# Last block of x turned as a full tile; SyncE's turns and loads planned with other durations

## Chip, cores, metric

One core of one Trainium2 chip. The metric is the device time of one launch in microseconds (us), lower is better; a kernel's figure is the median of its runs.

## The reference

Causal attention by blocks of 64 positions, and behind it a feed-forward layer with a swish. Inputs are f32.

```python
# q, k, v: (8 batches, 8 heads, 576 positions, 64)
scores = where(block_i >= block_j, q @ k.T / 8, -1e9)      # blocks of 64 positions
attn   = softmax(scores) @ v
x      = attn.transpose(0, 2, 1, 3).reshape(4608, 512)     # 8 * 576 rows, 8 * 64 columns
h      = x @ w_in                                          # (4608, 2048)
g      = h / (1 + exp(-beta * h))
out    = g @ w_out                                         # (4608, 512)
```

## The kernel before

**Units and row blocks.** The attention is cut into 32 units: unit u = 4b + c is the pair c of heads of batch b. The feed-forward layer is cut into nine row blocks r of 512 rows of x. A batch has 576 rows, so row block 3 (rows 1536 to 2047) needs all four units of batches 2 and 3, row block 4 those of batches 3 and 4, and so on.

**What a unit does.** Its q and k are loaded in f32 (L622 for the first two batches, L658 for the others, where one load brings two units), cast to bf16 by POOL (L629, L669) and turned so that the head dimension lies on the partitions: for batches 0 and 1 by TensorE (PE, L638) with a copy by VectorE (DVE), for batches 2 to 7 by one DMA transpose a pair of units, issued by SyncE (SP, L676). In this text that is a *q/k turn*, T0 to T11: T0 is for units 8 and 9, T1 for 10 and 11, and so on to T11 for 30 and 31. The pieces of v of a batch are loaded by SP too (L552, L555; six a batch from batch 1 on, the fifth and the sixth a quarter as large) and cast by POOL (L578, four casts a batch). Then come the scores on PE (L712, with a few at L443; from batch 2 on in three groups for two units: the first half of the first unit, a joint group, the first half of the second unit), the exponentials on ScalarE (ACT, L728 and L740), zeros into masked corners (DVE, L734 and L736), the product with v on PE (L768, 30 matmuls, here *AV*), and its division by the row sums on DVE (L780, L787), which gives x for the unit.

**How x gets its place.** x has 576 rows a unit and must be turned as well. For batches 0 to 2 (units 0 to 11) PE does it with five transposes (L817), the fifth of 64 rows. DVE or ACT copies the result to `xT`. For units 12 to 31 a DMA transpose on SP does it (L804), in one or two pieces: an *x turn*. Row block r on PE starts when the x of all its units is in `xT`.

**A row block.** Sixteen groups of four matmuls (L1004, 128x512 each) give h; each is followed by a tanh on ACT (L1014) and a product on DVE (L1018) that leaves g in `gT`. Row block 0 has plain output products (L1040, sixteen groups of four matmuls). Row blocks 1 to 8 use a Strassen-like form with 14 groups of eight matmuls of 256 columns (L925), whose sums of operands DVE makes (L889).

**What sets the order.** Nothing of this order stands in the code by hand. Every piece of work is an operation given to a planner with `P.op(engine, duration, emit, deps, tiles, prio, xfer=...)`. `Plan.schedule` (L85) plays the whole program through with these durations: at each moment an engine that is free takes the ready operation of best priority. For a DMA, `dur` is the time for which the issuing engine is held, `xfer` is the time that its data take in the ring of its queue, and the landing is put at the end of the transfer plus a constant (`LAND`, 2600 ns). An issue of SP that finds more than `RING` = 6000 ns of transfers ahead holds SP for longer (L269). What comes out is one fixed list for each engine, and each engine runs its list in order, waiting at semaphores. A duration that is changed therefore can change the place of every operation behind it, on all engines. Between the loads an order of their own is fixed (L842 to L851): q and k by units, and v of a batch behind its second pair of units.

**Buffers that matter here.** `ST` (four half buffers for q/k loads), one buffer of raw v for batches 2 to 7, two of cast v, three of `QKT`, three of `xq` (x before it is turned; the AV of unit u needs the x turn of unit u - 3 to have landed), and the eight banks of PSUM.

Of the kernel before, what the change touches and what calls it, by code (L numbers as in the profile page):

```python
# [359 lines left out]
def bass_blockwise_causal_attn__then__act_swish_beta_kernel(  # L360
# [10 lines left out]
    with es:  # L371
# [32 lines left out]
        xq = [sb(f"xq{i}", [128, 5, 128], bf16) for i in range(3)]  # L404
# [3 lines left out]
        identB = sb("identB", [128, 128], bf16)  # L408
# [8 lines left out]
        PSb = PS[:].rearrange("p b n -> p (b n)").bitcast(bf16).rearrange("p (b n) -> p b n", b=8)  # L417
# [3 lines left out]
        P = Plan()  # L421
# [16 lines left out]
        def pr(u):  # L438
            b, c = divmod(u, NPAIR)
            return u if b < 1 else 10 * u if b < 2 else 994 + 100 * (b - LAG) + 4.9 * c  # L440
# [11 lines left out]
        def xq_(tx):  # L452
            return 3 if tx.cls == "XX" else tx.slot
# [16 lines left out]
        for i in range(NQ):  # L470
# [5 lines left out]
            o = P.op("POOL", 200, mk(lambda g, i=i: g.memset(Vn[i][:, 4, :, 64:66], 0.0)), prio=-5)  # L476
# [6 lines left out]
        for i in range(NQ, NE + 1):  # L483
# [4 lines left out]
                  xfer=100, dma=("d_beta", 1), prio=0.1)  # L488
# [3 lines left out]
                  deps=[bt, c2], tiles=[tb], lat=400, mode="full", prio=5)  # L492
# [24 lines left out]
        for i in range(NFILL):  # L517
# [14 lines left out]
            n = 125  # L532
            o = P.op("PE", n, ff, deps=[c2, c4], tiles=[tf], lat=n, mode="full", prio=1e6 + i)
# [6 lines left out]
        for b in range(B):  # L540
            ts, t = P.tile("Vs"), P.tile("V")
# [3 lines left out]
            for h0, h1, e, tt in PARTS[b]:  # L545

                vs = []
                for i in tt:
                    def fv(g, e, ts=ts, t=t, b=b, h0=h0, h1=h1, i=i):
                        d = Vn[t.slot] if e == "POOL" else Vs[ts.slot]  # L550
                        if i < 4:
                            return [g.dma_start(d[:, i, h0:h1, 0:64],  # L552
                                                v[b, h0:h1, 128 * i:128 * i + 128, :].rearrange("h p d -> p h d"))]
                        o = i - 4
                        return [g.dma_start(d[64 * o:64 * o + 64, 4, h0 + o:h1:2, 0:64],  # L555
                                            v[b, h0 + o:h1:2, 512:576, :].rearrange("h p d -> p h d"))]

                    n = (h1 - h0) / 8 * (1 if i < 4 else 0.25)
                    if e == "SP":
                        o = P.op("SP", 300 + 550 * n, fv, tiles=[ts], xfer=1400 * n,  # L560
                                 prio=3.5 + 0.1 * (h0 > 0) if b == 0 else 4 * b + (3.5 if b < 2 else 0.5),
                                 dma=["d_V", h0, 1])
                    else:
                        o = P.op("POOL", 150 + 1450 * n, fv, tiles=[t], xfer=1400 * n, prio=-30 if b == 0 else 4 * b + (3.5 if b < 2 else 0.5), dma=["d_VP", h0, 1])
                        o.after = lastv if b else None
                    vs.append(o)
# [6 lines left out]
                n = 5 if 4 in tt else len(tt)  # L573
# [27 lines left out]

        xt = []
        early6 = []
        QKI, QKX = 550, 2700
        for u in range(NU):
            b, c = divmod(u, NPAIR)
            Tv = tl[b]
# [44 lines left out]
            elif p == 0:  # L652
# [23 lines left out]
                    return [g.dma_start_transpose(QKT[td.slot][:].rearrange("c a w (t n) -> c (a w t) n", n=128),  # L676
                                                  QKn[tn.slot][:].rearrange("p a w n -> p (a w n)")[:, 0:2560])]

                turned = [P.op("SP", 3250, ft, deps=casts, tiles=[tt_, tn], xfer=3200, prio=-1, dma=["d_T", 0, 1])]
            tqk, cps = tt_, turned  # L680
            ex = []
            zs = []
# [130 lines left out]

            def fx(g, e, tx=tx, px=px):
                for i in range(5):
                    r = 128 if i < 4 else 64
                    z = g.transpose(PSb[:, px.slot, 128 * i:128 * i + r], xq[xq_(tx)][0:r, i, :], identB[0:r, 0:r])  # L817
                return z

            xp = P.op("PE", 5 * 66, fx, deps=nrm, tiles=[tx, px], lat=5 * 66 + 170, mode="full", prio=pr(u)+.5 + 5 * (b < 1))  # L820

            def fy(g, e, px=px, c=c, b=b):
                for t0, n, x0 in pieces(b):
# [310 lines left out]
```

## Time and profile before

| what | us |
|---|---|
| median of 3 runs | 333.13 |
| lowest, highest run | 331.49, 333.41 |
| the profiled execution, its own time | 331.63 |
| its span, first to last instruction | 329.8 |
| PE busy in it | 318.9 (97%) |
| DVE, ACT, POOL busy | 223.9, 212.6, 87.1 |

The profile is of one execution at a granted TensorE clock of 1.000. A line of its views gives the start, the duration, the engine, the source line, the operation, and tiles as out<-in; what stands in brackets is idle time of the engine ahead of the group and what ended it. SPq is SyncE's sequencer, which issues DMAs; the duration there is that of the issue, not of the transfer.

### The profile page before, as it was taken

The numbers are of one execution on the slowest core, as the hardware profiler recorded it, in microseconds if no ns is written. First come the engines' busy times: TensorE is split into PE (matmuls) and PEld (weight loads), VectorE is DVE, ScalarE is ACT, GpSimd is POOL, SyncE is SP. The second block draws the span as 40 slices with busy tenths as digits, with TensorE's granted clock in tenths as the row PEclk, the third lists the DMA queues.
The fourth block names the chain that finished last, engine by engine and source line by source line (L and its number), as shares of the span: only waits on it lengthen the run. The fifth ranks groups of instructions, "written<-read, shape, count | busy, mean of one in ns | idle before, by whom it ended". The sixth has DMA issues, their size and how long they took to land.

```text
span 329.8 us, 7390 instructions
## 1 busy us (share of the span) xinstructions
PE 318.9 (97%) x3111; PEld 198.2 (60%) x3003; DVE 223.9 (68%) x448; ACT 212.6 (64%) x324; POOL 87.1 (26%) x127
## 2 busy tenths in 40 slices
PE   7999999999999999999999998999999999999996
PEld 1364455445687457855666655576566766666685
DVE  4848875678654899449957795678477685666742
ACT  2876974397557976678577675974876554544521
POOL 7756181065073045104530730250000000000000
PEclk9999999999999999999999999999999999999999
DMA  8999999999999999989989999969002320100023
GB/s 206 229 243 236 192 218 205 215 275 196 209 276 190 246 198 189 230 178 203 188 188 191 264 223 151 219 121 165 33 34 42 98 39 32 66 32 34 6 92 127
DMA packets 154993, 53.41 MB, mean 162 GB/s; under 512 B 139072, under 2 KB 154448, under 8 KB 154960
## 3 DMA queue, kind: packets, MB, share of 16 engines
q1 hardware_dynamic: 141200, 40.19, 64.5%
q0 software_dynamic: 5568, 4.36, 8.5%
q10 hardware_dynamic: 8192, 8.39, 8.0%
q8 instruction: 24, 0.39, 0.5%
q14 instruction: 9, 0.07, 0.1%
HBM read 36.71 MB, written 9.44 MB: 140 GB/s over the span
## 4 chain that ended last, share of the span: by engine, by line
PE 83%; ACT 4%; DVE 3%; POOL 3%; SPq 2%; DMA 2%; issue 2%; POOLq 0%; ACTq 0%
PE PS L1004 36%; PE PS L925 28%; PE PS L768 8%; PE PS L712 6%; PE PS L1040 4%; ACT E L728 3%; DMA Vs<-in_v_dram 2%; SPq L552 2%; DVE gT L1018 1%; POOL QKn L629 1%; ACT th L1014 1%; PE PS L817 1%; DVE OV L889 1%; PE PS L638 0%; POOL w_in L502 0%
## 5 line engine op out<-in xcount | busy, mean ns | idle before, releaser
L1014 ACT ACTIVATE th<-PS,beta 128x512 f32<-128x512 f32 x144 | 96.5, 700 | 60.3 <-PE PS L1004 59.1
L1004 PE MATMUL PS<-xT,w_in 128*128 128x512 bf16 x542 | 130.2, 379 | 3.7 <-ACT E L728 1.2
L1018 DVE SCALAR_TENSOR_TENSOR gT<-th,PS 128x512 f16<-128x512 f32 x144 | 95.1, 682 | 30.2 <-ACT th L1014 29.3
L728 ACT ACTIVATE E<-PS 128x1024 bf16<-128x1024 f32 x93 | 92.1, 1029 | 26.1 <-PE PS L712 25.7
L1004 PEld LDWEIGHTS PS<-xT,w_in 128*128 128x128 bf16 x576 | 53.2, 98 | 56.9 <-DVE gT L1018 2.5
L925 PE MATMUL PS<-w_out,gT 128*128 128x256 f16 x512 | 63.0, 273 | 0.0
L925 PEld LDWEIGHTS PS<-w_out,gT 128*128 128x128 f16 x512 | 49.0, 98 | 12.2 <-issue 1.5
L578 POOL CAST Vn<-Vs 128x640 bf16<-128x640 f32 (+1 forms) x28 | 22.4, 800 | 97.4 <-DMA Vs<-in_v_dram 96.1
L669 POOL CAST QKn<-ST 128x640 bf16<-128x640 f32 x48 | 37.9, 790 | 23.7 <-DMA ST<-in_q_dram 13.8
L712 PE MATMUL PS<-QKT 64*128 64x512 bf16 (+4 forms) x328 | 33.8, 295 | 0.4 <-ACT E L740 0.2
L768 PEld LDWEIGHTS PS<-Vn,E 128*128 128x128 bf16 x930 | 31.0, 97 | 4.3 <-issue 0.4
L946 ACT ACTIVATE ost<-PS 128x512 f32<-128x512 f32 x32 | 19.4, 606 | 21.7 <-PE PS L925 21.7
L925 PE MATMUL PS<-OV 128*128 128x256 f16 x256 | 32.0, 273 | 0.5 <-DVE OV L889 0.5
L768 PE MATMUL PS<-Vn,E 128*128 128x65 bf16 x930 | 32.0, 193 | 0.3 <-POOL Vn L578 0.3
L712 PEld LDWEIGHTS PS<-QKT 64*128 64x128 bf16 (+1 forms) x328 | 13.3, 96 | 27.0 <-issue 7.8
L925 PEld LDWEIGHTS PS<-OV 128*128 128x128 f16 x256 | 24.1, 98 | 6.5 <-issue 0.8
L787 DVE TENSOR_TENSOR xq<-PS,inv 128x640 bf16<-128x640 f32 x30 | 24.7, 822 | 0.8
L889 DVE TENSOR_TENSOR OV<-gT 128x1024 f16<-128x1024 f16 x32 | 24.0, 757 | 1.1 <-PE PS L925 0.6
L734 DVE MEMSET E<- 64x64 uint32 x62 | 6.9, 112 | 20.5 <-ACT E L728 18.3
L949 DVE SCALAR_TENSOR_TENSOR ost<-PS,ost 128x512 f32<-128x512 f32 x22 | 15.2, 689 | 8.2 <-PE PS L925 5.8
L925 PE MATMUL PS<-OV,gT 128*128 128x256 f16 x128 | 16.1, 273 | 0.0
L1040 PE MATMUL PS<-w_out,gT 128*128 128x512 f16 x64 | 15.5, 380 | 0.0
(64 smaller groups left out, 175.3 us busy)
## 6 DMA issues: line engine op xcount, KB each, us to landing
out_dram<-ost ACTq DMA_DIRECT2D x32, 256.0 KB, 2.9
ST<-in_q_dram SPq DMA_DIRECT2D x12, 576.0 KB, 6.2
ST<-in_k_dram SPq DMA_DIRECT2D x12, 576.0 KB, 7.6
Vs<-in_v_dram SPq DMA_DIRECT2D x24, 256.0 KB, 4.5
ST<-in_q_dram SPq DMA_DIRECT2D x8, 288.0 KB, 6.5
ST<-in_k_dram SPq DMA_DIRECT2D x8, 288.0 KB, 7.0
w_in<-in_moe_w_in_dram POOLq DMA_DIRECT2D x4, 512.0 KB, 10.1
w_out<-in_moe_w_out_dram POOLq DMA_DIRECT2D x4, 512.0 KB, 9.9
```

Of the source, the lines that this page charges most:

```text
L578: return g.tensor_copy(Vn[t.slot][:, 0:n, g0:g1, 0:64], Vs[ts.slot][:, 0:n, g0:g1, :])
L669: return g.tensor_copy(QKn[tn.slot][:].rearrange("p a w n -> p (a w n)")[:, 640 * (2 * a + w):][:, 0:640] .rearrange("p (t h d) -> p t h d ...
L712: z = g.matmul(o, QKT[tqk.slot][r, uu % 2, 1, 128 * t + y:128 * t + m + y], x)
L728: return g.activation(E3[es_(te)][:, g0, :, :], PS[:, ps.slot:ps.slot + 2, :], ACT.Exp, scale=0.125)
L768: z = g.matmul(o, eblk(te, t, i, h), Vn[Tv.slot][:, t, 2 * c + h, 0:65], start=(t == 0), stop=(t == i))
L787: return g.tensor_tensor(xq[xq_(tx)][:].rearrange("p i (h d) -> p h i d", h=2), both(pv, 0, 64), x, ALU.mult)
L889: return P.op("DVE", dve_t(SZ * HC / 2), mk(lambda g: g.tensor_tensor(fo(), fx(), fy(), op)), deps=deps, tiles=tiles, prio=prio)
L925: x = g.matmul(PS[:, pw.slot, HM * w:HM * w + HM], fa()[:, j, 128 * w:128 * w + 128], fb()[:, j, :], start=first and (pair or w == 0) and ...
L1004: z = g.matmul(PS[:, ph.slot, :], w_in[:, c, 128 * j:128 * j + 128], xT[:, c, row % RX:row % RX + RC], start=(c == 0), stop=(c == 3))
L1014: return g.activation(th[tt.slot][:], PS[:, ph.slot, :], ACT.Tanh, scale=beta[:, j:j + 1])
L1018: return g.scalar_tensor_tensor(out=gT[tg.slot][:, j, :], in0=th[tt.slot][:], scalar=1.0, in1=PS[:, ph.slot, :], op0=ALU.add, op1=ALU.mult)
L1040: z = g.matmul(PS[:, po.slot, 0:d1 - d0], gT[tg.slot][:, j, 128 * w:128 * w + 128], w_out[:, j, d0:d1], start=(j == 0), stop=(j == NJ - 1))
```

## The change

Four numbers of the planner and one piece of code.

- The fifth transpose of an x tile on PE (units 0 to 11) takes all 128 rows instead of 64. Only the first 64 columns of its result are used, as before. The planner's duration goes from 5 x 66 to 5 x 57 ns.
- A q/k turn: SP is held for 4200 ns instead of 3250, and its transfer takes 2600 ns instead of 3200.
- A q/k load of two units (`QKX`): its transfer takes 2300 ns instead of 2700.
- A whole piece of v (256 KB) from batch 1 on: 1100 ns instead of 1400.

```diff
-                        o = P.op("SP", 300 + 550 * n, fv, tiles=[ts], xfer=1400 * n,
+                        o = P.op("SP", 300 + 550 * n, fv, tiles=[ts], xfer=(1400 if b < 1 else 1100) * n,
...
-        QKI, QKX = 550, 2700
+        QKI, QKX = 550, 2300
...
-                turned = [P.op("SP", 3250, ft, deps=casts, tiles=[tt_, tn], xfer=3200, prio=-1, dma=["d_T", 0, 1])]
+                turned = [P.op("SP", 4200, ft, deps=casts, tiles=[tt_, tn], xfer=2600, prio=-1, dma=["d_T", 0, 1])]
...
             def fx(g, e, tx=tx, px=px):
                 for i in range(5):
-                    r = 128 if i < 4 else 64
-                    z = g.transpose(PSb[:, px.slot, 128 * i:128 * i + r], xq[xq_(tx)][0:r, i, :], identB[0:r, 0:r])
+                    z = g.transpose(PSb[:, px.slot, 128 * i:128 * i + 128], xq[xq_(tx)][:, i, :], identB[:])
                 return z

-            xp = P.op("PE", 5 * 66, fx, deps=nrm, tiles=[tx, px], lat=5 * 66 + 170, mode="full", prio=pr(u)+.5 + 5 * (b < 1))
+            xp = P.op("PE", 5 * 57, fx, deps=nrm, tiles=[tx, px], lat=5 * 57 + 170, mode="full", prio=pr(u)+.5 + 5 * (b < 1))
```

What comes out of the planner differs as follows. PE's list is the same, but for the fifth transposes, up to the 13th h group of row block 0 (43.6 us in the profile before); there the AVs of units 4 and 5 come two h groups earlier. SP's list is the same up to the third of the six pieces of v of batch 2; from there on:

```
SP before: v (third) | T0 | v x3 | q k q k | v | T1 | v v | T2 | v x3 | q k q k | v | T3 | v | T4 | x12 | v x4 | q | x13 | k q | x14 | k |
           v | T5 | x15 | v | T6 | x16 x17 | v x4 | q k | x18 | q k | v | x19 | T7 ...
SP after:  v (third) | v x3 | T0 | q k q k | v | T1 | v v v | T2 | v v | q k q k | v v | T3 | v | T4 | v x3 | q k | x12 | q k | x13 | T5 |
           v v | x14 | T6 | v x4 | q | x15 | k q k | x16 | T7 | v x4 | x17 | v v | q k | T8 | x18 x19 ...
```

Here v is a piece of v, q and k are loads of two units, T is a q/k turn, and x12 is the x turn of unit 12. POOL's list differs in one place, late: two casts of q come ahead of the casts of v of batch 6.

On PE the groups are the same ones in another order. The places that the prediction speaks of: the scores of unit 10, which wait for T1, stand behind 14 of the sixteen h groups of row block 1, where before they stood behind all sixteen, and behind three more output groups of row block 0 (L1040), one L925 group and the five transposes of unit 9 as well. The first h group of row block 3 stands right behind the AV of unit 16, where before six L925 groups, the AV of unit 17 and two groups of scores came in between.

## The prediction

> **What bounds the kernel now.** I read the page's first part, then busy time by stretches, then PE's own waits, and last SP and POOL in order of time between 60 and 137 us, because every line that is changed moves them.
>
> ```profile
> PE 318.9 (97%) x3111; PEld 198.2 (60%) x3003; DVE 223.9 (68%) x448; ACT 212.6 (64%) x324; POOL 87.1 (26%) x127
> ...
> 43.50:100.00 56.50, 55.85 (x558) 32.83 (x550) 39.14 (x85) 33.21 (x50) 23.20 (x30) 1.00 1.19 227
> 100.00:190.00 90.00, 89.10 (x937) 57.15 (x923) 64.30 (x132) 67.08 (x101) 29.26 (x36) 1.00 1.06 206
> 190.00:232.00 42.00, 39.65 (x379) 25.06 (x374) 30.52 (x57) 28.74 (x43) 9.87 (x12) 1.00 0.99 170
> 232.00:320.00 88.00, 87.48 (x710) 59.02 (x713) 59.45 (x103) 50.64 (x77) 0.00 (x0) 1.00 0.16 47
> ```
>
> After the name of the stretch and its length, the first figure is PE's busy time: 55.85 of 56.50, 89.10 of 90.00, 39.65 of 42.00. PE is the bound and its list hardly waits. The last figure is GB/s: 227 up to 100 us, 47 from 232 us on. The loads fill the first 230 us and then are over.
>
> ```profile
> 197.59 1.05 PE L925 MATMUL PS<-OV 128*128 128x256 f16 x8 [0.48 <-DVE OV L889]
> 201.55 0.81 PE L1004 MATMUL PS<-xT,w_in 128*128 128x512 bf16 x3 [1.21 <-ACT E L728]
> ...
> L1004 PEld LDWEIGHTS PS<-xT,w_in 128*128 128x128 bf16 x44 | 3.9, 98 | 5.4 <-DMA xT<-xq 1.3 <-DVE gT L1018 0.3 <-issue 0.2
> ```
>
> These are the only two stalls of note. The second is the start of row block 5 and belongs to an x turn, as PE's weight loads from 195 to 220 us say (`DMA xT<-xq 1.3`). With three small ones (0.2 to 0.3 each, at 52, 98 and 219 us) all stalls behind 43 us come to 0.6 + 1.25 + 0.8 = 2.7 us. That is the most that a better order can win there.
>
> ```profile
> 76.30 4.29 SPq L676 DMA_TRANSPOSE QKT<-QKn  x1
> ...
> 89.26 2.80 SPq L658 DMA_DIRECT2D ST<-in_k_dram  x1
> ...
> 97.57 2.50 SPq L552 DMA_DIRECT2D Vs<-in_v_dram  x1
> 100.17 5.10 SPq L676 DMA_TRANSPOSE QKT<-QKn  x1
> ...
> 106.00 4.30 SPq L676 DMA_TRANSPOSE QKT<-QKn  x1
> ...
> 129.69 5.08 SPq L676 DMA_TRANSPOSE QKT<-QKn  x1
> 134.82 1.29 SPq L804 DMA_TRANSPOSE xT<-xq  x1
> 136.55 0.37 SPq L552 DMA_DIRECT2D Vs<-in_v_dram  x1
> 136.98 5.10 SPq L676 DMA_TRANSPOSE QKT<-QKn  x1
> ```
>
> A q/k turn holds SP for 4.3 to 5.1 us. T1 starts at 76.30, T5 at 129.69, and the x turn of unit 15 directly behind it at 134.82. By the landing times of their own DMAs (median row of the view of each line) T1 lands 7.3 us after its issue, at 83.6, and that x turn 4.5 after, at 139.3.
>
> ```profile
> 70.87 1.51 POOL L669 CAST QKn<-ST 128x640 bf16<-128x640 f32 x2
> 73.69 1.84 POOL L669 CAST QKn<-ST 128x640 bf16<-128x640 f32 x2 [1.31 <-DMA ST<-in_k_dram]
> 76.40 1.51 POOL L669 CAST QKn<-ST 128x640 bf16<-128x640 f32 x2 [0.87 <-DMA ST<-in_q_dram]
> 79.10 1.69 POOL L669 CAST QKn<-ST 128x640 bf16<-128x640 f32 x2 [1.19 <-DMA ST<-in_k_dram]
> ```
>
> POOL waits for each load, so its starts are the landings: 73.69 - 70.87 = 2.8, then 2.7 and 2.7 us a load. The planner took 2.7 for it and takes 2.3 now. Where loads come one after another, the new figure is too short.
>
> **What the Trainium skill says.** "TensorEngine Tiling (Array Packing)", Key Properties: "Changing tiling mode (not just tile) drains the TensorE". The trace agrees: two x tiles of five transposes each start at 82.81 and the next group at 83.72, 0.455 us a tile, while five full ones should take 5 x 55 ns = 0.27 (the L925 matmuls of 256 columns run eight in 0.87 us, so 128 columns take 55 ns: an estimate). "DMA: Bandwidth & Descriptors", Anatomy of one DMA: DMA engines do not wait at semaphores; the wait is held on the issuing sequencer. So a turn that waits on SP holds every load behind it. SP shows it: at 117.59 it had idled 1.0 us for the x of unit 13, at 125.04 2.2 us for unit 14. Same page, Queues, rings and completion order: descriptors of a ring are consumed in ring order, so a transfer put ahead delays the next. T0, issued at 51.65 into a full ring, landed 12.7 us later.
>
> **The change part by part.**
>
> *Fifth tile full.* A tile followed by work of 128 rows saves 0.455 - 0.27 = 0.18 us. Of units 4 to 11, five are (4, 6, 7, 8, 9): 0.9 us. Units 5, 10 and 11 were followed by scores, which are of 64 rows anyway; there the drain only moves, 0.1 us each lost. Net -0.6 us. Units 0 to 3 lie where PE waits for POOL's casts (25 to 28 us): nothing.
>
> *The old stalls.* Each of the five places has another neighbour now: at F4 (197 us) and row block 5 (201 us) more groups stand between. All gone: -2.7 us. Together with the tile -3.3.
>
> *T0 behind three pieces of v.* They take 1.1 + 0.3 + 0.3 us of transfer and up to 2 us in the ring, so T0 lands at 65.7 to 67.4 instead of 64.3. Its scores (67.75 before) stand two groups of 0.87 earlier and are due at 65.4. A wait of 0.3 to 2 us; it is contained in the next one.
>
> *T1.* Ahead of it stand the same loads as before (v, T0 and four q/k loads, one v), and its casts wait for the same landings, so it lands at 83.6 again, or up to 1 us sooner since no gap is left around T0: I take 83.1. The scores of unit 10 lie five h/L1040 groups (0.87 each), one L925 group (0.87) and one x tile (0.45) earlier: 86.43 - 5.67 = 80.8, less 0.2 (old stall) and 0.6 (tiles) = 80.0. PE, and all that its list holds behind, waits 3.1 us.
>
> *Row block 3.* It needs the x turn of unit 15. Its first h group stood at 141.8. Six L925 groups, an AV (0.91) and two score groups (0.66 each) now come later: 141.8 - 7.5 = 134.3; less old stalls 0.45 and tiles 0.6, plus the 3.1 of T1: due at 136.4. SP's list up to that turn, with the durations of before's rows: the q/k loads end at 97.0 (before 97.5); v 2.5 and 1.5; T3 5.1; v 0.6; T4 4.3 (111.0); three v 2.4; q, k 2.4; x turn 1.3; q, k 2.4; x turn 1.3: 120.8. T5 then waits for POOL. The last v, issued at 113.4, lands some 4 us later; four casts of v (3.75) and four of q and k (3.3, the last load landing at 120 to 121) end at 124.3. T5 4.3 to 5.1, two v 2.0, x turn 1.2, T6 4.3 to 5.1, four v 3.3, q 0.6: the x turn of unit 15 is issued at about 139 (137 without any throttling, 141.5 with all of it). It lands 2.7 to 4.5 later: 139.7 to 146. I take 141.5: a wait of 5.1 us. The x itself is ready at 129.3 (its AV at 126.1, and 3.2 to the end of L787, as before); what delays it is SP: before, it came directly behind T5; now six v, the turn of unit 14, T6 and a load lie between.
>
> *Row block 4.* Due at 163.7 + 8.2 = 171.9. From the turn of unit 15 to that of unit 19 SP issues seven q/k loads and v by pairs and fours, T7, T8 and four x turns of two pieces, some 32 us: it lands at about 172.7. Wait 0.8, bounds 0 to 3. Behind it the list has 3 us to spare at row block 5 and 1 at row block 7, and the loads end sooner than before: nothing.
>
> *Sum.* 3.1 + 5.1 + 0.8 = 9.0 of new waits, -3.3 saved: +5.7 us. Against the profiled execution's own 331.63: 337.3. The median of the runs shown lies 1.5 above that execution; half of it added, 338.0.
>
> **Rivals.**
>
> - *A: the first wait only.* T1 is late, but SP reaches the turn of unit 15 early (137.3, landing 139.7; the wait is 139.7 - 136.4 = 3.3, or 1.5 where T1 cost PE more). For it: SP idles less at x turns than before. Against: T5 needs four loads' casts. -3.3 + 3.1 + 1.5 to 3.3 = +1.3 to +3.1: 333 to 335.
> - *B: SP throttled throughout.* T6 and v each take their longer durations, the turn lands at 146, row block 4 waits 3: 3.6 + 9.0 + 3 - 3.3 = +12.3: 344.
> - *C, the other side: the DMAs keep ahead.* The queue before was issued later than need be, and the loads, asked for earlier, land earlier. T1 must land by 80.0 and the turn of unit 15 by 133.3; then only the -3.3 stays: 328.3, or 330 with small new stalls. Against: four q/k loads 2.7 us apart stand before T1 at 227 to 240 GB/s; it decides only if those come at 2.0. It turns to slower when the two waits together pass 3.3 us.
>
> That the lists do not change is excluded: SP, PE and POOL differ as listed.
>
> **How the numbers follow.** Forecast 0.47, A 0.25, B 0.15, C 0.13. The range runs from C with small stalls to B: 331.0 to 343.5; the likeliest case's own range, from the bounds of the two landings, is 335 to 341. A change of about 1% is what a measurement of this kernel can tell (its three runs span 0.6%). Slower by over 1% (336.5): most of the forecast and B, 0.58. Within: A, the low end of the forecast and half of C, 0.37. Faster by over 1% needs the whole of C: 0.05.
>
> **What would show it.** Right: in PE's list a gap of about 3 us at the first scores behind h group 14 of row block 1, released by T1 (near 83), and one of 3 to 9 us at the first h group of row block 3, near 141, released by the turn at L803; POOL's starts on q/k loads still 2.7 us apart; no stall left at row block 5; a pitch of x tiles near 0.28. Wrong: T1's scores at 80 without a gap, or row block 3 starting by 137; or waits of ACT and DVE in place of DMAs.

## The result, and the profile after

| | before | changed |
|---|---|---|
| median of the runs made together, us | 332.78 | 351.66 |
| lowest, highest | 331.49, 333.41 | 350.57, 353.69 |
| ratio to before, 95% interval | | 1.058, 1.0515 to 1.0644 |
| the profiled execution's own time, its span | 331.63, 329.8 | 350.76, 349.0 |

The changed kernel is 5.8% slower; forecast were 338.0 us and a range up to 343.5. A ratio leaves out runs that lie more than 1.5% above the fastest of their own kernel (ten of 22 of kernel 3, none of the kernel before beside it), so it need not be the quotient of the medians, and the profiles of kernels 3, 7 and 13 are of such longer runs. In the tables below "ratio" is always to the kernel before on the same chip.

The first part of the page and its slices, each slice now 8.7 us:

```profile
PE 323.2 (93%) x3145; PEld 198.7 (57%) x3003; DVE 224.1 (64%) x448; ACT 212.9 (61%) x324; POOL 87.0 (25%) x127
...
PE   7898999897999998089998999999999999999996
...
PEclk9999999999999999569999999999999999999999
DMA  8999999999899999999989996080311220020023
```

PE is no longer busy without a break: there is a 0 in the 17th slice (140 to 148 us), and its clock was halved from there into the next slice. The DMA engines stay at 8 or 9 up to about 210 us, as before. The same three stretches as before, in the order PE, PEld, DVE, ACT, POOL, clock, DMA share, GB/s:

```profile
43.50:100.00 56.50, 52.87 (x538) 29.87 (x525) 40.04 (x84) 33.83 (x51) 24.02 (x30) 1.00 1.14 217
100.00:190.00 90.00, 75.83 (x758) 47.29 (x739) 52.68 (x106) 53.66 (x81) 30.26 (x40) 0.92 1.08 207
190.00:232.00 42.00, 42.00 (x421) 26.26 (x408) 28.73 (x58) 31.86 (x47) 8.82 (x11) 1.00 0.79 154
```

PE lost 13.3 us more between 100 and 190 us (89.10 busy before, 75.83 now) and 3.0 between 43.5 and 100. From 190 to 232 us PE is busy throughout. The waits of PE for DMAs, largest first (total, times, longest), and then their places in PE's list; idle time and its releaser stand in brackets:

```profile
PE PS L1003 <- DMA xT<-xq: 12.5, 2, 10.9
PE PS L712 <- DMA QKT<-QKn: 3.6, 2, 1.9
```

```profile
68.05 0.39 PE L712 MATMUL PS<-QKT 64*128 64x512 bf16 x2 [1.72 <-DMA QKT<-QKn]
...
84.59 0.39 PE L712 MATMUL PS<-QKT 64*128 64x512 bf16 x2 [1.91 <-DMA QKT<-QKn]
...
137.94 1.08 PE L768 MATMUL PS<-Vn,E 128*128 128x65 bf16 x30 [0.39 <-DVE E L736]
149.94 3.59 PE L1003 MATMUL PS<-xT,w_in 128*128 128x512 bf16 x8 [10.92 <-DMA xT<-xq]
...
185.12 1.25 PE L1003 MATMUL PS<-xT,w_in 128*128 128x512 bf16 x5 [1.61 <-DMA xT<-xq]
```

Those released by a DMA are the four places that the prediction had named (T0, T1, row block 3, row block 4), each with the releaser that it had named. The third is twice as long as forecast. Its first eight matmuls also took 3.59 us, where the same group takes 1.89 elsewhere. The reason stands in the clock, the last figure but two:

```profile
130.00:140.00 10.00, 8.22 (x99) 6.01 (x94) 6.54 (x13) 5.20 (x8) 1.78 (x2) 1.00 1.20 200
140.00:150.00 10.00, 0.07 (x1) 0.07 (x2) 0.14 (x1) 0.00 (x0) 2.95 (x5) 0.54 1.07 208
150.00:160.00 10.00, 10.00 (x68) 4.67 (x65) 3.89 (x9) 6.66 (x9) 6.15 (x8) 0.78 1.24 208
```

SP from T3 on (start, length of the issue):

```profile
103.23 5.29 SPq L676 DMA_TRANSPOSE QKT<-QKn  x1
...
109.25 3.38 SPq L676 DMA_TRANSPOSE QKT<-QKn  x1
...
115.49 4.53 SPq L658 DMA_DIRECT2D ST<-in_k_dram  x1
120.06 3.27 SPq L804 DMA_TRANSPOSE xT<-xq  x1
...
125.64 3.25 SPq L804 DMA_TRANSPOSE xT<-xq  x1
128.93 4.10 SPq L676 DMA_TRANSPOSE QKT<-QKn  x1
...
136.56 3.33 SPq L676 DMA_TRANSPOSE QKT<-QKn  x1
139.95 1.70 SPq L552 DMA_DIRECT2D Vs<-in_v_dram  x2
141.69 2.48 SPq L555 DMA_DIRECT2D Vs<-in_v_dram  x2
144.21 0.61 SPq L658 DMA_DIRECT2D ST<-in_q_dram  x1
144.86 2.81 SPq L804 DMA_TRANSPOSE xT<-xq  x1
...
178.52 5.45 SPq L804 DMA_TRANSPOSE xT<-xq  x4
```

The x turn of unit 15 is issued at 144.86, behind T6, four pieces of v and a load, and by the completion of its own DMA it landed at 149.89; its x had been ready since 131.1. The last line holds the turns of units 18 and 19; that of unit 19 landed at 185.07, where before it had landed at 167.98. Row block 4 starts right behind it in both, at 185.12 and at 168.50. From that landing to the end of the span the changed kernel takes 163.9 us, and the kernel before 161.8. So nearly the whole loss can be read as that one turn's delay of 17 us, although PE's list shows only 1.6 us of waiting at it.

### The profile page after: what moved, and what is told of

It reads as the page before. It is cut to its first block, busy times and chain, and to the rows that moved or that the text cites. A ratio compares the mean times of both kernels' runs of the same rounds, so it can differ in the third digit from the quotient of the medians.

```text
span 349.0 us, 7423 instructions
## 1 busy us (share of the span) xinstructions
PE 323.2 (93%) x3145; PEld 198.7 (57%) x3003; DVE 224.1 (64%) x448; ACT 212.9 (61%) x324; POOL 87.0 (25%) x127
## 4 chain that ended last, share of the span: by engine, by line
PE 67%; SPq 16%; DMA 8%; DVE 3%; POOL 3%; issue 1%; ACT 1%; POOLq 0%
PE PS L1003 28%; PE PS L924 26%; SPq L552 10%; PE PS L768 6%; PE PS L712 5%; SPq L555 3%; SPq L658 3%; DMA Vs<-in_v_dram 2%; DMA xT<-xq 2%; DMA QKT<-QKn 2%; DMA ST<-in_k_dram 1%; PE PS L1039 1%; DVE gT L1017 1%; DVE gT L888 1%; DVE OV L888 1%
## 5 line engine op out<-in xcount | busy, mean ns | idle before, releaser
L1003 PE MATMUL PS<-xT,w_in 128*128 128x512 bf16 x576 | 140.1, 383 | 12.5 <-DMA xT<-xq 12.5
L712 PE MATMUL PS<-QKT 64*64 64x64 bf16 (+4 forms) x328 | 34.1, 297 | 4.3 <-DMA QKT<-QKn 3.6
L578 POOL CAST Vn<-Vs 128x640 bf16<-128x640 f32 (+1 forms) x28 | 23.3, 831 | 54.2 <-DMA Vs<-in_v_dram 52.7
L712 PEld LDWEIGHTS PS<-QKT 64*128 64x128 bf16 (+1 forms) x328 | 13.3, 96 | 33.0 <-DVE gT L1017 6.5
L646 DVE COPY QKT<-PS 128x576 bf16<-128x576 bf16 x16 | 12.0, 756 | 5.2 <-PE PS L638 4.9
```

Source lines behind the costliest of these rows:

```text
L578: return g.tensor_copy(Vn[t.slot][:, 0:n, g0:g1, 0:64], Vs[ts.slot][:, 0:n, g0:g1, :])
L712: z = g.matmul(o, QKT[tqk.slot][r, uu % 2, 1, 128 * t + y:128 * t + m + y], x)
L1003: z = g.matmul(PS[:, ph.slot, :], w_in[:, c, 128 * j:128 * j + 128], xT[:, c, row % RX:row % RX + RC], start=(c == 0), stop=(c == 3))
```

## The experiments

The reference of all of them is the changed kernel (351.66) or the kernel before. Landing times are those of the DMAs' own completions. Edits are shown shortened; `moved(late, ahead)` puts operations of SP's list directly behind `ahead`. SP's queue is called full where SP is held at its issues by the transfers ahead. In the tables "X15" and "X19" are the landings of the x turns of units 15 and 19.

**1. Unit 15's turn first.** Theory A: one turn stands too far back on SP. Theory B: SP's list is full, and the time comes back at the next turn.

```diff
+        sp, x14, x15 = P.order["SP"], xt[14], xt[15]
+        moved(sp[sp.index(x14) + 1:sp.index(x15)], x15)   # T6, four v, one q behind unit 15's turn
```

> The changed kernel (351.7 us) with one move on SP: T6, the four pieces of v and the q/k load that stand between the x turns of units 14 and 15 are put behind the x turn of unit 15. Theory A (that one turn stands too far back in SP's list, and nothing else): it is issued near 134 and landed near 138, row block 3 starts near 138 instead of 149.9, its wait falls from 10.9 to about 1 us, TensorE keeps its full clock there, and the time falls by about 13 us to 337 to 339. Theory B (SP's list is full from 62 to 185 us, so what is taken from one wait comes back at the next turn): the x turn of unit 19 still lands near 183 to 185, row block 4 waits some 12 us in row block 3's place, and the time stays at 348 to 352.

Measured: 355.26 us, ratio 1.0655 (1.0584 to 1.0726). PE's list of this kernel:

```profile
138.72 1.90 PE L1003 MATMUL PS<-xT,w_in 128*128 128x512 bf16 x8 [0.41 <-DMA xT<-xq]
...
161.35 1.42 PE L768 MATMUL PS<-Vn,E 128*128 128x65 bf16 x30 [3.15 <-DMA xT<-xq]
...
185.05 1.46 PE L1003 MATMUL PS<-xT,w_in 128*128 128x512 bf16 x3 [10.93 <-DMA xT<-xq]
```

Row block 3's wait fell from 10.92 to 0.41 us, as both theories have it, and nothing was won: 3.15 came at the AV of unit 19 (which needs the `xq` buffer that the turn of unit 16 frees) and 10.93 at row block 4, which started at 185.05, in the changed kernel at 185.12. A falls, B holds in the places, but the time lies 3 us above its range. Behind 185.05 the span goes on for 166.0 us instead of 163.9. The long wait and with it the halved clock (178.9 to 189.2 us) now lie at row block 4, where some 4 us of work at half the clock cost 2; this agrees, but was not tested by itself.

**2. Keep PE busy in the wait.**

```diff
+        def fwarm(g, e):
+            for i in range(50):
+                z = g.matmul(PS[:, h3.tiles[0].slot, :], identB[:], w_in[:, 0, 0:512])
+            return z
+        # placed right ahead of row block 3's first h group; needs no x turn
```

> The changed kernel with 50 additional matmuls of 512 columns right ahead of row block 3's first h group, into the PSUM bank that this group overwrites; they need no x turn, so PE is busy while SP's turn is on its way. They are additional work and change no output. The x turn still lands near 149.9. Theory A (the granted clock fell to one half from 140.8 to 154.4 because PE stood still, and that cost about 2.3 us of PE's work behind the wait): the clock stays at 1.0, the span falls by about 2 us to near 349.5. Theory B (the lowered clock lies in the wait itself and costs nothing): no change, 351 to 352. If the matmuls last longer than the wait, up to 1 us is lost.

Measured: 351.65 us, ratio 1.0566 (1.0493 to 1.0639). From PE's list:

```profile
137.81 10.96 PE L1068 MATMUL PS<-w_in,identB 128*128 128x512 bf16 x50
148.60 1.89 PE L1003 MATMUL PS<-xT,w_in 128*128 128x512 bf16 x8
...
183.38 3.32 PE L1003 MATMUL PS<-xT,w_in 128*128 128x512 bf16 x8 [3.88 <-DMA xT<-xq]
```

The clock stays at full speed at row block 3 (1.89 instead of 3.59 us for eight matmuls), so it was PE's idleness that halved it. The turn of unit 15 landed at 148.5, just before the added matmuls ended. But row block 4 then waits 3.88 instead of 1.61 us for unit 19's turn and is itself slowed (3.32). The time is the one that B gave, but not for B's reason: the lowered clock had cost PE about 2 us, and the next late turn hid them.

**3. The full fifth tile alone**, in the kernel before, with all planner numbers as before, so that the lists stay.

```diff
-                    r = 128 if i < 4 else 64
-                    z = g.transpose(PSb[:, px.slot, 128 * i:128 * i + r], xq[xq_(tx)][0:r, i, :], identB[0:r, 0:r])
+                    z = g.transpose(PSb[:, px.slot, 128 * i:128 * i + 128], xq[xq_(tx)][:, i, :], identB[:])
```

> The kernel before with the full fifth x tile as the only edit; all planner numbers stay, so every engine's list is the same as before. Expected from the drain that goes at five of the twenty x tiles, 0.18 us each, less 0.1 us each at three where it only moves: 0.6 us faster than before, 0.2%, 332.2 where before has 332.8. The rival, that the full tile costs nothing and wins nothing because its neighbours hide it: within 0.1%.

Measured: 333.77 us against 333.46, ratio 0.9973 (0.9942 to 1.0005). The ratio lies near the forecast of 0.2%, but its interval includes no gain at all, and the medians of all runs point the other way. A gain in the whole is not shown. The tile is not what costs.

**4. More x turns first.**

```diff
+        moved(sp[sp.index(xt[14]) + 1:sp.index(xt[15])], xt[15])
+        ahead = [xt[17], xt[18], xt[19]]       # directly behind xt[16]; T7, T8, v and loads behind them
+        moved([o for o in sp[sp.index(xt[16]) + 1:sp.index(xt[19])] if o not in ahead], xt[19])
```

> The changed kernel with the x turn of unit 15 directly behind that of unit 14, and the x turns of units 17, 18 and 19 directly behind that of unit 16, so that T6, T7, T8, nine pieces of v and three q/k loads come behind the x turns that they stood ahead of. Theory B (SP is full, and the planner's new order spends its time on loads and turns of later batches while x turns wait): both waits, at row blocks 3 and 4, fall below 1.5 us, and the time is 334 to 338. Theory A (only unit 15 was late): the same time as with unit 15's turn alone. A third way: T7 and T8 are now late for their own scores and the wait moves to TensorE's score groups of the last batches, 340 to 346.

Measured: 352.32 us, ratio 1.0581 (1.0512 to 1.065). Unit 19's turn landed at 169.9, 15 us sooner, and the wait was still there, now in front of AVs:

```profile
PE PS L768 <- DMA xT<-xq: 12.0, 2, 8.1
```

The two are 3.9 us at the AV of unit 19 (turn of unit 16) and 8.1 at that of unit 23 (turn of unit 20, which now has T7, T8, five loads and twelve pieces of v between it and the turn of unit 19). The numbers of B and of the third way missed; the time is near that of kernel 1, as A's wording has it, but A had fallen there. What is put right for one turn returns at the next that was not moved.

**5 and 6. SP's list alone, in both directions.** In the changed kernel SP's list is replaced by that of before; in the kernel before, by that of the changed kernel. Every other list stays.

```diff
+        listed = [523, 527, 26, 547, ...]      # the other kernel's order of SP's operations
+        byidx = {o.idx: o for o in P.order["SP"]}
+        P.order["SP"] = [byidx[i] for i in listed]
```

> The changed kernel with one engine's list replaced: SP issues its loads and turns in the order of the kernel before. The lists of TensorE, ScalarE, VectorE and GpSimd, the buffers and the full fifth tile stay those of the changed kernel. Theory B (what costs the time is that SP's list puts loads and turns of later batches ahead of x turns): the turn of unit 15 lands near 139 and that of unit 19 near 168 again; the changed PE list wants them some 7 and 4 us earlier than the list before did, so waits of about 3 us at the scores of unit 10 (the turn T1) and 2 to 3 us at row block 3 stay, less the 3.3 us saved by tile and old stalls: 333 to 337. Theory C (PE's changed list is what costs, whatever SP does): 345 or more.

> The reverse: the kernel before, with SP's list alone in the order of the changed kernel; all other lists, the buffers and the partial fifth tile stay those of before. Theory B (SP's order makes the loss): the turn of unit 15 lands near 149, that of unit 19 near 184, row blocks 3 and 4 wait 7 to 8 us each, and the time is 346 to 351, nearly that of the changed kernel. Theory C (PE's list makes it): within 3 us of before, 331 to 336.

| | time, us | ratio (95%) | X15 | X19 |
|---|---|---|---|---|
| before | 332.12 | | 139.3 | 168.0 |
| before with the changed SP list | 349.67 | 1.0501 (1.0441 to 1.0561) | 149.4 | 184.3 |
| changed with SP's list of before | 342.78 | 1.0311 (1.0244 to 1.0378) | 138.6 | 173.4 |
| changed | 351.66 | 1.058 (1.0515 to 1.0644) | 149.9 | 185.1 |

PE's waits, first in the kernel before with the changed SP list, then in the changed kernel with SP's list of before:

```profile
PE PS L1004 <- DMA xT<-xq: 14.5, 2, 7.4
```

```profile
PE PS L1003 <- DMA xT<-xq: 5.9, 4, 4.5
PE PS L712 <- DMA QKT<-QKn: 3.6, 1, 3.6
```

The changed SP list alone makes nearly the whole loss, as B has it (7.4 and 7.1 us of waiting at row blocks 3 and 4). Giving SP its old list back wins only 9 of 19 us, where 15 to 19 were expected: the changed PE list asks for T1 and for unit 19's turn earlier, and where PE is late itself, SP, which waits for x at its turns in that order, is held too (unit 19's turn issued at 169.1, before at 163.9). So SP's list is the larger part, and PE's changed list costs as well where SP does not keep up with it.

**What the plan says.** The planner gives each operation a start. Set against the trace, the chip's issue less the plan's start of the same turn, in us:

| turn | before | changed | v back | q/k back | turns back |
|---|---|---|---|---|---|
| T1 | -2.0 | 5.4 | 2.7 | 1.9 | 5.2 |
| unit 15 | -2.2 | 14.4 | 9.9 | 8.3 | 11.5 |
| unit 19 | -0.9 | 18.7 | 8.5 | 14.1 | 15.0 |
| unit 23 | -0.4 | 18.6 | 14.1 | 15.0 | 23.2 |

Before, the chip ran ahead of its plan by 0.4 to 2.2 us at these turns. In the changed kernel it falls behind by up to 19: the plan lets SP prefetch q, k and v of later batches because it believes that it has the time. Nor did the plan promise a gain: by the planner's own times the program ends at 337.1 us with the changed numbers and at 337.0 with those of before. The last three columns are the next experiments.

**7, 8 and 9. One planner number taken back.**

```diff
-                        ... xfer=(1400 if b < 1 else 1100) * n
+                        ... xfer=(1400 if b < 1 else 1400) * n              # 7: v
-        QKI, QKX = 550, 2300
+        QKI, QKX = 550, 2700                                              # 8: q/k load
-                turned = [P.op("SP", 4200, ft, ..., xfer=2600, ...)]
+                turned = [P.op("SP", 3250, ft, ..., xfer=3200, ...)]      # 9: q/k turn
```

> The changed kernel with one planner number taken back: the transfer of a piece of v from the second batch on is 1400 again in place of 1100; QKX 2300, the turns' 4200 and 2600 and the full tile stay. The plan then puts 91 operations ahead of the x turn of unit 19 on SP, where the changed kernel has 97 and before 88, and 80 ahead of that of unit 15 as in the changed kernel (before 73). Theory B (each operation that SP issues ahead of an x turn delays it by some 1.9 us: 17.1 us for nine): unit 15's turn lands near 149 and row block 3 waits about 10 us, unit 19's lands near 174 and row block 4 waits nothing more: 344 to 348. If v's number alone were the cause: 333 to 336.

> The changed kernel with one planner number taken back: QKX, the transfer of a q or k load, is 2700 again in place of 2300; the rest of the change stays. The plan puts 75 operations ahead of the x turn of unit 15 (before 73, changed 80) and 97 ahead of that of unit 19 (before 88, changed 97). Theory B (count of operations ahead on SP): no wait of note at row block 3, the turn of unit 19 lands at 183 to 185 and row block 4 waits 10 us or more: 346 to 351. If the too short load duration were the cause of the loss, as the reading of GpSimd's 2.7 us a load would have it: 333 to 337.

> The changed kernel with one planner pair taken back: a q/k turn costs 3250 on SP and 3200 of transfer again in place of 4200 and 2600; QKX 2300, v's 1100 and the full tile stay. The plan then issues the x turn of unit 15 at 130.3 and that of unit 19 at 162.2, with 75 and 93 operations ahead of them (changed kernel 80 and 97, before 73 and 88). Theory D (each new number is smaller than what the queue spends on such a transfer when it is full, so any two of them still make a plan that runs ahead of the chip): the chip issues unit 19's turn 9 to 14 us behind the plan, as with v's or q/k's number taken back, waits of 5 to 9 us at row blocks 3 and 4 follow, and the time is 342 to 349. If the turns' pair alone made the loss: 332 to 336.

| taken back | time, us | ratio (95%) | X15 | X19 |
|---|---|---|---|---|
| v | 347.55 | 1.041 (1.0316 to 1.0504) | 152.5 | 178.2 |
| q/k load | 348.67 | 1.0445 (1.0334 to 1.0556) | 144.8 | 186.0 |
| q/k turn | 355.09 | 1.0677 (1.0615 to 1.0739) | 144.5 | 180.9 |

The waits of PE for x turns, in the same order:

```profile
PE PS L1003 <- DMA xT<-xq: 16.8, 2, 12.8
```

```profile
PE PS L1003 <- DMA xT<-xq: 12.8, 2, 9.8
```

```profile
PE PS L1003 <- DMA xT<-xq: 19.1, 3, 9.0
```

Taking back any one number is not enough: at the turns of units 15 to 23 the plan still runs 8 us or more ahead of the chip, and most of the loss stays. With v's number taken back row block 4 waited for nothing, as forecast, but the second wait (4.0 us) came at row block 5, where none was. With the q/k number taken back I had expected no wait at row block 3 from the count of operations alone. It waited 9.8 us: 75 operations stood ahead of unit 15's turn, two more than before, but these are a q/k turn and a whole piece of v, some 5 us by the prices of the next experiment (an estimate). The turn landed at 144.8, 5.4 us later than before, and PE, by a list that had changed with it, was there at 135. Counting operations without their kinds was too simple; with the turns' pair taken back, the loss came out 6 us above the upper bound.

**10 and 11. Planner numbers from the full queue.** While SP's queue is full, what an operation costs is the spacing of landings, not the time from its issue to its landing. From 100 to 200 us, and 62 to 82, a landing less that of the operation before it on SP (where it was issued before that landing), mean over the stretch, in the profiles of the kernel before, the changed one and kernels 1 to 8 (lowest to highest, in brackets their mean):

| | measured, us | plan before | plan changed |
|---|---|---|---|
| q or k load of two units | 2.8 to 3.1 (2.9) | 2.7 | 2.3 |
| piece of v, mean of four whole and two quarter ones | 1.0 to 1.4 (1.2) | 1.05 | 0.83 |
| q/k turn | 2.8 to 3.8 (3.4) | 3.2 | 2.6 |
| x turn | 0.9 to 1.6 (1.3) | 1.1 | 1.1 |

With these prices the loss can be counted from the lists alone. Ahead of unit 19's turn SP has 97 operations instead of 88: two q/k turns, two loads, three whole and two quarter pieces of v more. That is some 18 us (an estimate from the means in the table), and the turn landed 17.1 us later. Ahead of unit 15's turn stand 80 instead of 73, one q/k turn, one load and the same five pieces more: some 12 us, measured 10.6.

```diff
-        QKI, QKX = 550, 2300                  # v 1100; turn 4200 on SP, 2600 of transfer
+        QKI, QKX = 550, 2900                  # 10: v 1200; turn 4400, 3300
+        QKI, QKX = 550, 2900                  # 11: v 1200; turn 4300, 3000; x turn 1500 (was 1100)
```

> The changed kernel with planner numbers taken from the spacing of landings while SP's queue is full (100 to 200 us, all runs so far): q or k load 2900 (measured 2.8 to 3.1 us), v piece 1200 (1.0 to 1.3), q/k turn 4400 on SP (issue 4.2 to 4.6) and 3300 of transfer (2.6 to 4.0); the full tile stays. The plan issues the x turn of unit 15 at 131.9 (71 operations ahead) and that of unit 19 at 169.2 (88 ahead, as before). Theory D (a plan that runs ahead of the chip makes the loss): the chip issues both within 4 us of the plan, no wait of PE passes 3 us, and the time is 331 to 337. If instead any other order is bad (theory E: the order of before is a lucky one): x turns are still 8 us or more behind the plan and 342 or more.

> The changed kernel with the planner's numbers again from the full queue: q or k load 2900, v piece 1200, q/k turn 4300 on SP and 3000 of transfer, and now the x turn too, 1500 of transfer in place of 1100 (spacing of landings measured 1.0 to 1.6); the full tile stays. This plan ends 3.5 us sooner than the first one with such numbers (335.4 against 338.9 in the planner's time) and has row blocks 4 and 5 at 169.2 and 207.5 where that one has 174.0 and 216.1. Theory D (once the numbers fit the full queue the chip follows the plan): turns within 2 us of the plan, no x turn waited for by more than 2 us, 330 to 333, the same as before or 1 us better through the tile. If the fit of the first one was an accident: turns 4 us or more behind the plan and 336 or more.

| | time, us | ratio (95%) | chip less plan: T1, units 15, 19, 23 |
|---|---|---|---|
| 10 | 334.98 | 1.0086 (1.0052 to 1.012) | 0.3, -0.7, 0.0, 0.1 |
| 11 | 332.36 | 0.9993 (0.9971 to 1.0016) | 2.0, -0.6, 1.5, 0.6 |

SP in 10 (unit 15's turn is in the first line, unit 19's in the second), and then PE's stretch from 100 to 190 us and its waits in 11:

```profile
127.33 5.17 SPq L804 DMA_TRANSPOSE xT<-xq  x2
...
169.22 3.11 SPq L804 DMA_TRANSPOSE xT<-xq  x2
```

```profile
100.00:190.00 90.00, 87.85 (x896) 55.39 (x882) 62.59 (x131) 68.35 (x100) 27.79 (x36) 1.00 1.16 201
```

```profile
PE PS L1003 <- DMA xT<-xq: 0.8, 1, 0.8
...
PE PS L712 <- DMA QKT<-QKn: 0.6, 1, 0.6
```

With such numbers the chip follows the plan within 2 us at these turns, and 17 to 19 us of loss are gone. Both times came in as theory D had them; in 10 one wait, 3.6 us at row block 4, passed its limit of 3. The second is as fast as the kernel before; that it is faster is not shown. The counts ahead of the turns of units 15 and 19 are again within two of those of before (71 and 88 in 10, 72 and 86 in 11), although the order is another. So another order than that of before is not bad as such; the one from prices that were too low is.

**12. The turns' pair alone**, in the kernel before (with the full tile):

```diff
-                turned = [P.op("SP", 3250, ft, ..., xfer=3200, ...)]
+                turned = [P.op("SP", 4200, ft, ..., xfer=2600, ...)]
```

> The kernel before with the turns' pair of planner numbers alone changed (4200 on SP and 2600 of transfer in place of 3250 and 3200) and the fifth x tile turned full, still priced at 66 ns in the plan; QKX 2700 and v's 1400 as before. The plan issues unit 15's x turn at 139.5 and unit 19's at 165.8, with 75 and 90 operations ahead. Theory D: the other numbers are generous enough that the chip stays within 4 us of the plan, as before's own plan (0.4 to 4 us ahead of it), and the time is 331 to 336. Theory E (any new order loses): 342 or more.

Measured: 338.21 us, ratio 1.0182 (1.0115 to 1.025), a miss by 2 us for D and by more for E. The chip stayed within 0.5 us of the plan at T1 and the turns of units 15 and 19, and within 3.1 at unit 23. One wait of 3.3 us remained, at row block 3: the plan has unit 15's turn land at 144.8 and PE begin at 145.1, but PE was there at 142.0 and the turn landed at 144.85. So it is not enough that SP keeps to the plan: PE, which ran 3 us ahead of it, then waits. v's number and the load's alone, in the kernel before, were not run.

**13 to 16. What is full: SP's issue or the transfers?** In 13 the pieces of v of batches 4 to 7 go to ScalarE's queue. In 14 and 15 half of these pieces is left out, by rows and by heads, with the same instructions. In 16 they move the same bytes with twice the instructions.

```diff
+            o.eng, o.dma = "ACT", ["d_W", *o.dma[1:]]                               # 13
+                            r = 64 if b >= 4 else 128        # rows of each piece   # 14
+                            h2 = h0 + 4 if b >= 4 else h1    # heads of each piece  # 15
+                                    for x0, x1 in (((h0, h0 + 4), (h0 + 4, h1)) ... # 16, two DMAs a piece
```

> The changed kernel with the 24 pieces of v of batches 4 to 7 taken off SP's list and issued by ScalarE on its own queue, 10 us later than planned; all else, and SP's order of what is left, as in the changed kernel. Theory B1 (SP's issue is what is full: it spends about 1 us on each piece): SP reaches the x turn of unit 15 about 8 us and that of unit 19 about 14 us earlier, the waits at row blocks 3 and 4 fall below 4 us, 333 to 340. Theory B2 (the DMA engines are what is full: the same bytes must go before, whatever queue they take): the pieces on the other queue take their share, SP's loads and turns land as late as before, unit 19's turn at 180 or later, 346 to 352. ScalarE may be held by the issues, up to 3 us more in either.

> The changed kernel with each 128-row piece of v of batches 4 to 7 loading only its first 64 rows (half of these batches' v is left out); the number and order of all instructions stay on every engine. Ahead of the x turn of unit 15 stand 8 such pieces, ahead of that of unit 19 twelve. Theory B2 (the DMA engines' transfers are what is full, and SP only waits for room in the ring): each halved piece frees some 0.7 us, so unit 15's turn lands 5 to 6 us earlier (near 144) and unit 19's 8 to 9 us (near 176.5), and the time falls by 6 to 9 us, to 342 to 346. Theory B1 (SP's own issue is what is full: an instruction costs the same, whatever it moves): both land as before, within 2 us, and the time stays at 350 to 353.

> The changed kernel with each 128-row piece of v of batches 4 to 7 loading four of the eight heads, on all 128 rows (half of these batches' v is left out); count and order of all instructions stay. Halving by rows moved unit 15's turn by 1.8 us and unit 19's by 3.1 us only, but half of the rows may use fewer of the DMA engines. Theory B2 (transfers are what is full): with all rows in use each of 8 and 12 halved pieces frees 0.5 to 0.7 us, unit 15's turn lands near 145 and unit 19's at 177 to 179, 343 to 346 us. Theory B1 (SP's own issue is what is full): both as with half of the rows or later, 148 to 150 and 182 to 185, and 347 to 352.

> The changed kernel with each 128-row piece of v of batches 4 to 7 issued as two DMAs of four heads each: the same bytes, and SP issues 8 more instructions ahead of the x turn of unit 15 and 12 more ahead of that of unit 19, each some 0.6 us when SP is not held. Theory B1 (issue is what is full): unit 15's turn lands some 5 us later (near 155), unit 19's some 7 us later (near 192), 356 to 360. Theory B2 (transfers): no change beyond 1.5 us, 350 to 353.

| | time, us | ratio (95%) | T1 lands | X15 | X19 |
|---|---|---|---|---|---|
| changed | 351.66 | 1.058 (1.0515 to 1.0644) | 84.5 | 149.9 | 185.1 |
| 13: v on ScalarE's queue | 361.41 | 1.0777 (1.0681 to 1.0873) | 89.9 | 154.8 | 195.0 |
| 14: half of v, by rows | 347.25 | 1.043 (1.0362 to 1.0499) | 84.7 | 148.1 | 182.0 |
| 15: half of v, by heads | 346.70 | 1.0371 (1.0329 to 1.0413) | 86.5 | 147.0 | 181.3 |
| 16: v in two DMAs a piece | 353.13 | 1.0577 (1.0531 to 1.0624) | 81.9 | 148.7 | 184.7 |

T1 lies ahead of every piece that these edits touch, and it lands at different times in these profiles. So X15 and X19 are better counted from T1. Kernel 16 speaks most plainly: twelve more instructions on SP ahead of unit 19's turn, and counted from T1 it lands 2.2 us later, where B1 had 7. In 13 SP has up to 18 instructions fewer ahead of that turn, and it lands 10 us later, where B1 had 14 earlier. Of these 10 us, 5.5 were there at T1 already, ahead of the first piece that was moved, and the profile is of the longest of four runs (364.52; the others took 356.18 to 362.84). One q/k turn held SP for longer than any in the changed kernel:

```profile
177.95 10.79 SPq L676 DMA_TRANSPOSE QKT<-QKn  x1
```

So SP's own issuing is not what is full; it is held by what its issues must wait for. In the changed kernel SP issues for 82 of the 85 us from 100 to 185; if each of these 47 issues took the shortest time that its kind takes in 13 of the profiles (2.9 us a q/k turn, 1.2 an x turn, 0.6 a load, 0.4 a piece of v), they would take 44, an estimate. That v on another queue freed nothing agrees with the Trainium skill, "DMA: Bandwidth & Descriptors", Issuing engines are not separate DMA queues, which has DMAs of all issuing engines run on the same 16 DMA engines and interleave. Counted from T1, half of v by heads moved the turns of units 15 and 19 by 5.0 and 5.8 us, close to what B2 had (5, and 6 to 8), and half by rows by 2.0 and 3.3 us, where B2 had 5 to 6 and 8 to 9. Why half of the rows frees less than half of the heads is open, and so is why 13 lost time rather than nothing; its time lies above B2's range.

## Why the prediction was wrong, step by step

- *The bound, the places, the releasers*: right. The wait of DVE and ACT that would have spoken against it did not come; POOL's starts on loads are still 2.7 us apart, as the timeline of POOL shows (the next one comes 2.4 behind these). Of the prediction's own three spacings the first, 2.8, began at a cast that had waited for POOL and not for a load; the other two hold.

```profile
71.78 1.50 POOL L669 CAST QKn<-ST 128x640 bf16<-128x640 f32 x2 [3.98 <-DMA ST<-in_q_dram]
74.48 1.50 POOL L669 CAST QKn<-ST 128x640 bf16<-128x640 f32 x2 [1.20 <-DMA ST<-in_k_dram]
77.20 1.50 POOL L669 CAST QKn<-ST 128x640 bf16<-128x640 f32 x2 [1.22 <-DMA ST<-in_q_dram]
```

- *Fifth tile full, -0.6*: the pitch fell from 0.455 to 0.28 us (a tile at 81.38, the next group at 81.66), as worked out; a gain in the whole is not shown (kernel 3).
- *The old stalls, -2.7*: row block 5 has none left, as forecast, but three small waits for DVE's operand sums and masks came in new places (0.57, 0.56 and 1.0 us at 134, 137 and 181 us), so what was gained here is nearly given back.
- *T0 and T1, 3.1 together*: T0's wait was 1.8 us (0.3 to 2 forecast), T1's 2.0, sum 3.8. These and the waits below are counted start to start, from where the next group would have begun at the usual pitch, which differs from the idle time in brackets by up to 0.2 us. T1 landed at 84.5 where 83.1 was taken.
- *Row block 3, 5.1*: this is the step that failed, and it failed in the walk of SP's list.

| point of the walk | forecast | measured |
|---|---|---|
| T4 issued, end | 111.0 | 112.6 |
| x turn of unit 13, end | 120.8 | 128.9 |
| T5 begins | 124.3 | 128.9 |
| x turn of unit 15 issued | 139 | 144.9 |
| it lands | 141.5 | 149.9 |

  From T4's end to the end of the turn of unit 13 the walk has 9.8 us and the chip took 16.3. Three pieces of v, four loads and two x turns stand there. I priced a pair of loads at 2.4 and an x turn at 1.3. The v and one pair of loads took what the walk has; the other pair took 2.8 us more (4.53 for its k load alone), and the two x turns together 3.9 more (3.27 and 3.25). The price of 1.3 came from x turns that stood directly behind a q/k turn (units 12 and 15) or behind a wait (unit 14). In the changed list those of units 12 and 13 stand directly behind a k load, and for this place the kernel before had another row:

```profile
110.34 1.28 SPq L804 DMA_TRANSPOSE xT<-xq  x1
...
180.30 1.89 SPq L658 DMA_DIRECT2D ST<-in_k_dram  x1
182.23 3.65 SPq L804 DMA_TRANSPOSE xT<-xq  x1
```

  Over 100 to 200 us the mean issue of an x turn rose from 2.28 to 3.21 us. The wait of T5 for POOL, which the walk had put in, did not happen. The walk's end also has two slips: its terms behind 124.3 add to 140.0 to 141.6, not 139, and issue to landing was taken as 2.5, below its own range of 2.7 to 4.5, and measured as 5.0. By its own terms the wait would have been 6.3 to 9.7 us. The turn landed 8.4 us later than forecast. PE came 2.5 us later than forecast too (0.7 at T0 and T1, 1.1 in the waits for DVE; the rest was not traced); 5.1 + 8.4 - 2.5 = 11.0, which is the wait measured start to start. What would have served is the count in 10 and 11: seven operations more ahead of the turn, each at the spacing of landings.
- *Row block 4, 0.8*: 1.7 us measured, within its bounds of 0 to 3, but by luck. The turn of unit 19 was put at 172.7 and landed at 185.1, the largest error of the whole walk; 8.4 of these 12.4 us were there at unit 15. That it cost so little is because row block 3 had already made PE late. Kernel 1 shows it: with row block 3's wait gone it all came back here. Row blocks 3 and 4 are not two terms to be added; the later landing sets the end, and the earlier wait is only a part of it.
- *Not foreseen*: TensorE's halved clock from 140.8 to 154.4 us, some 2.3 us of PE's work, which kernel 2 shows to be hidden behind unit 19's turn; and a wait of 0.7 us at 272.
- *Sum*: 3.8 + 11.1 + 1.7 + 2.1 + 0.7 + 2.3 = 21.7 of new losses, less the 3.3 that were to be saved, makes 18.4; the spans differ by 19.2.
- *Rivals*: A is out: SP reached unit 15's turn at 144.9, not at 137.3. B (SP throttled throughout) was the nearest, but priced from the longest rows of before, 12.3 us, it was still 7 short. C, that the loads land earlier because they are asked for earlier, is out: T1 landed 0.8 us later than before, not 3.6 earlier. The prediction's remark that 2.3 us for a load is too short was the cause in small. I used it for T1 only and then walked SP's list with prices of the same kind.

## What to carry to other kernels

In this kernel's full queue the price of a transfer was the spacing of landings (2.8 to 3.1 us for a load that was put at 2.3), and the planner, told less, moved prefetches ahead of what was needed next. Count first what a new list puts ahead of the operation that a later stage waits for, and price it so. Compare the plan's start times with the trace at a few late operations: a gap that grows from one to the next says more than any single wait. And a wait at one stage is no measure of what its removal wins as long as a later stage waits for the same queue.

## What was not expected of the hardware

- How long an x turn holds SP depends on what stands directly ahead of it. In 17 traces, from 62 to 200 us, an issue right behind another turn took 1.2 to 2.5 us (median 1.3, 126 issues), and one right behind a q or k load 2.4 to 5.7 (median 3.3, 68 issues). In the changed kernel's full queue too, those of units 18 and 19, behind T8, took 1.2 to 1.6.
- TensorE's clock was halved from 140.8 us, some 1.8 us behind its last matmul, to 154.4, about 4.5 us after it had resumed. In kernel 1 it fell 4.8 us after the last matmul at row block 4, and in kernel 2 0.3 us after PE had resumed (183.7). In each trace the changes of the clock lie whole multiples of 3.41 us apart (in the changed kernel 133.12 and 13.65).
- The Trainium skill, "TensorE: Matmul & The Clock Gate", Part 1, gives one idle window of about 3.4 us that runs freely; the steps of 3.41 agree, but the window need not be idle. In the changed kernel matmuls fill 37% of the 3.41 us ahead of 140.8. In all 18 traces together they fill at most 40% of the step ahead of each of the 28 falls, and at least 43% of each of the 1688 steps at full clock that no fall followed; the matmuls' ends are modelled, so these shares are estimates. T1's wait of 1.9 us in the changed kernel left 46% of its step busy, and the clock stayed; the same wait in kernel 4, 2.1 us, left 39%, and it fell.
